# A delta-rule attention with a feed-forward layer on one core: loads of the attention moved between two weight loads in SyncE's queue

## The chip, the cores and the metric

One core of a Trainium2 chip. The metric is the device time of one execution in microseconds (us); of several runs the median is given. The profile is of one execution, taken by the hardware profiler.

## What is computed

A recurrent attention (the delta rule) over 4 sequences, 8 heads, 768 steps and head size 48, and behind it a feed-forward layer of 384 to 2048 to 384 with a leaky relu, on 3072 rows:

```python
for t in range(S):
    kt, vt, bt = (k_n[:, :, t], v[:, :, t], beta[:, :, t, None])   # k_n: k over its norm
    y[:, :, t] = np.einsum('bhd,bhde->bhe', q[:, :, t], state)
    v_old = np.einsum('bhde,bhd->bhe', state, kt)
    state = state + bt[:, :, :, None] * np.einsum('bhd,bhe->bhde', kt, vt - v_old)
...
h = x @ w_in
g = np.maximum(0.01 * h, h)
return (g @ w_out)
```

## The kernel before

The 768 steps are cut into 12 blocks of 64. Within a block the recurrence becomes products of matrices with the inverse of a triangular matrix, so that only the state goes from block to block. Each block is done in two groups (`g`) of two sequences. Blocks are numbered from 0 here as in the code; blocks 0 and 1 share one inverse.

The stages of a block `n`, each a generator: `gram(n)` loads `kq` (k and q, transposed, two loads for each group), multiplies k by k and k by q on TensorE (L306), copies the first product with ScalarE to `gs` (L310), stores the half-blocks of it that lie on the diagonal to a buffer `gd` in DRAM, four stores for each group (L314), and at the end reads `gd` back in another layout as `L`, two loads (L344). `inv` takes the norms from `L`'s diagonal on VectorE (`norms`, from L363) and eliminates step by step on VectorE (L387, L392); the inverse goes through DRAM (`td`, `tt`) and back (`rt`, `sq`), unless it is that of blocks 0 and 1. `solve(n)` applies it: `load` (with `merge_z`, TensorE's `pz`, L489), `tie`, `kt` (scales `v` on VectorE, L626), `step_w`, `step_y` (takes `q`) and `step_s` (the state into the next block's `v`). `ffn(n)` is the feed-forward layer, 16 pieces of 128 hidden units; it is the bulk of TensorE's work (L721, L712). From block 1 on its operands are split in a high and a low part, `xl` (L124), `gl` (L736) and the weights' lows (L189) being made by VectorE.

The weights come as eight loads of 1.5 MB, wr0 to wr7, each a "pair" of two pieces (`load_w(j)`). During block 0 each is packed by ScalarE (`pack`, L148), converted by VectorE (`conv`, L158 to L161), expanded by ScalarE (L168) and finished by VectorE (`final`, L175), and later split (`cast`, `lows`). Loads 4 to 7 wait for a memset on VectorE (L131), which writes to the same buffer and is placed behind a mark.

The order on every engine is chosen by a planner in the framework, which lets each engine take the earliest traced instruction that its own estimate of the times has ready. `with behind(name)` adds an edge: what is traced in it stays behind the instruction that `mark[name]` holds at that time, on that instruction's engine, without a wait. `mark["kq"]` orders SyncE's loads: before the change it is the last load of `qx` for blocks 0 and 1, from the first 12 us, until much later in the kernel. So all `kq`, `rk`, `rv`, `rq` loads (the tiles of k, v and q) are free to go as soon as their buffers are. `fetch(n, g)` issues the three loads of a group of block `n`. The buffers of `v` and `q` are four each (two blocks), those of `k` two (one block). For block 1 and block 2 `fetch` is called in `solve(n)`'s `load`, for later blocks at the end of the solve of the block before.

The core of the order by hand, at the end of the kernel's body: the first stages, then a loop over the 17 steps of each block's `ffn`, in which `work` lists weight steps by number (`load_w` of 6 and 7 in steps 2 and 4) and `weave_at` interleaves the other generators.

Of the kernel before, what the change touches and what calls it, by code (L numbers as in the profile page):

```python
# [12 lines left out]
U16 = mybir.dt.uint16  # L13
# [13 lines left out]
NGR = NSEQ // GS  # L27
# [20 lines left out]
def delta_moe_kernel(ctx: ExitStack, tc, kq0, kqT, kv, qT, beta, cst, w_all, out, nblk):  # L48
# [10 lines left out]
    nc = tc.nc  # L59
    DO = out.shape[1]  # L60
    NFC = w_all.shape[1] // (2 * DO)
    w16 = w_all.bitcast(U16)
# [25 lines left out]
    UP, DN = slice(0, D), slice(R0, P)  # L88
# [4 lines left out]
    def of(x, n, g):  # L93
        return ring[x][(n * NGR + g) % NR[x]]

    def tv(n, g):

        t = of("t", n, g)
        return t.rearrange("p y (c v) t -> p c y v t", c=2) if n < 2 else t.rearrange("p c (y v) t -> p c y v t", y=2)
# [16 lines left out]
    raws, mark = {}, {}  # L116

    def behind(name):

        return tc.issue_after(mark[name]) if name in mark else nullcontext()  # L120
# [5 lines left out]
    def load_w(j, gate=None):  # L126
        if j < NJ:
            raws[j] = raw = sb.tile([P, 8 * DO], F32, tag=f"w{j}", name=f"wr{j}", bufs=1)
            if gate:
                with behind(gate):  # L130
                    nc.vector.memset(raw[:, 0:1], 0.0)  # L131
            with behind("kq"):
                nc.sync.dma_start(raw.bitcast(U16), w16[:, 16 * DO * j + 1:16 * DO * (j + 1) + 1])

    def signs():
        nc.scalar.mul(neg, eye, -1.0)
# [13 lines left out]
    def after(inst):  # L150
        mark["gl"] = mark["dv"] = inst.ins
# [11 lines left out]
    def expand(j, gate, e=slice(0, 2)):  # L163

        g = parts[j][0]
        a, b = e.start * 2 * DO, e.stop * 2 * DO
        with behind(gate):
            nc.scalar.copy(g[:, a:b], g.bitcast(BF16)[:, 4 * DO + a:4 * DO + b])  # L168

    def final(j, e=slice(0, 2)):  # L170
        g, mid = parts[j]
        a, b = e.start * 2 * DO, e.stop * 2 * DO
        gi = g[:, a:b].bitcast(U32)
        with behind("dv"):
            after(nc.vector.scalar_tensor_tensor(gi, mid[:, a:b], 13, gi, ALU.logical_shift_right, ALU.bitwise_or))  # L175
        for e in range(e.start, e.stop):
            w32[2 * j + e] = g[:, e * 2 * DO:(e + 1) * 2 * DO]
# [19 lines left out]
    def need(gen, fn, n):  # L197
        while (fn, n) not in done:
            next(gen)
# [354 lines left out]
    LD = 2  # L554
    NSLOT = LD + 4

    def fetch(n, g):
        with behind("kq"):
            for i, x in enumerate("kv"):
                nc.sync.dma_start(of(x, n, g)[DN].rearrange("p h u t -> p (h u t)"), kv[n, g, i])  # L560
            nc.sync.dma_start(of("q", n, g)[UP].rearrange("p h u t -> p (h u t)"), qT[n, g])

    nts = {}

    def lengths(n):

        b, i = where[n]
        ps = ps_a.tile([P, 512], F32, tag="a", name=f"pn{n}")
        nc.tensor.matmul(ps[DN, 0:HS], nrm[b][i * 64:i * 64 + 64], eye0[i * 64:i * 64 + 64], start=True, stop=True)
        nt = nts[n] = sb.tile([P, NGR, 2, GU], F32, tag="nt", name=f"nt{n}", bufs=2)  # L570
        if n < 2:
            for y in range(2):
                nc.scalar.copy(nt[DN, :, :, y * NPAIR:(y + 1) * NPAIR],
                               ps[DN, y * GH:(y + 1) * GH].rearrange("p (g h v) -> p g h v", g=NGR, h=2))
        else:
            nc.scalar.copy(nt[DN].rearrange("p g h u -> p (g h u)"), ps[DN, 0:HS])
        if not n:
            for g in range(NGR):
                v = of("v", n, g)
                for u in range(GU):  # L580
                    for c in range(2):
                        nc.scalar.mul(v[DN, c, u], v[DN, c, u], nt[DN, g, c, u:u + 1])

    def solve(n):
        b = where[n][0]
        need(iv, inv, b)
        if n not in nts:
            with behind("po"):
                lengths(n)
        nt = nts.pop(n)  # L590

        def load(g):
            merge_z(n, g, tv(n, g))
            if 0 < n < 3:
                fetch(n, g)

        def tie(g):
            merge_u(n, g, tv(n, g))

        def heads(rows):  # L600

            return ((c, u, slice(c * 64, c * 64 + rows)) for u in range(GU) for c in (1, 0))

        def quarters():

            return ((c, u, e) for u in range(GU) for c in range(2) for e in range(2))

        def out_of(x, g, w):
            p = ps_a.tile([P, 512], F32, tag="a", name=f"{x}{n}_{g}")
            return p[:, 0:GU * w].rearrange("p (u t) -> p u t", u=GU)  # L610

        def kt(g):

            t, k, v = tv(n, g), of("k", n, g), of("v", n, g)
            if n:
                pv = out_of("pk", g, C)
                for c, u, r in heads(D):
                    nc.tensor.matmul(pv[r, u], k[DN, c, u], t[DN, c, u // NPAIR, u % NPAIR], start=True, stop=True)  # L618
                for c in range(2):
                    nc.scalar.mul(t[UP, c], pv[c * 64:c * 64 + D].rearrange("p (y v) t -> p y v t", y=2), -1.0)  # L620
            if not n:
                return
            for s in range(GS):
                us = slice(s * NPAIR, (s + 1) * NPAIR)
                with behind("gl"):
                    nc.vector.tensor_tensor(  # L626
                        v[DN, :, us], v[DN, :, us],
                        nt[DN, g, :, us].rearrange("p h (u o) -> p h u o", o=1).broadcast_to([C, 2, NPAIR, D]), ALU.mult)

        def step_w(g):  # L630
            t, v = tv(n, g), of("v", n, g)
            pv = out_of("pw", g, D)
            for c, u, e in quarters():
                a = c * C + e * HC
                nc.tensor.matmul(pv[a:a + HC, u], t[:, c, u // NPAIR, u % NPAIR, e * HC:(e + 1) * HC], v[:, c, u], start=True, stop=True)  # L635
            for c in range(2):
                d = nc.scalar.copy(v[DN, c], pv[c * 64:c * 64 + C])  # L637
            mark["rv"] = d.ins

        def step_s(g):  # L640
            k, v, v1 = of("k", n, g), of("v", n, g), of("v", n + 1, g)
            pv = out_of("pc", g, D)
            for c, u, r in heads(D):
                with nullcontext() if n else behind("ph"):
                    nc.tensor.matmul(pv[r, u], k[:, c, u], v[:, c, u], start=True, stop=True)  # L645
            for c in range(2):
                nc.scalar.copy(v1[UP, c], pv[c * 64:c * 64 + D])  # L647

        def step_y(g):

            qa, v = of("q", n, g), of("v", n, g)
            pv = ps_a.tile([P, 512], F32, tag="a", name=f"py{n}_{g}")
            for c, u, e in quarters():
                a = (c ^ (u // NPAIR)) * C + e * HC
                nc.tensor.matmul(pv[a:a + HC, u * D:(u + 1) * D], qa[:, c, u, e * HC:(e + 1) * HC], v[:, c, u], start=True, stop=True)  # L655
            ys[n, g] = y = sb.tile([P, DO], F32, tag="ys", name=f"ys{n}_{g}", bufs=3)
            mark["ys"] = nc.scalar.copy(y, pv[:, 0:DO]).ins
            if not n and not g:
                expand(0, "ys", slice(1, 2))

        stages = [(0, load), (1, tie), (LD, kt), (LD + 1, step_w), (LD + 2, step_y), (LD + 3, step_s)]
        if n in (0, nblk - 1):
            stages.remove((LD + 3, step_s))
        for s in range(NSLOT):
            for g in range(NGR):
                for at, stage in stages:
                    if at == s:
                        stage(g)
            if s == NSLOT - 1:
                done.add((solve, n))  # L670
                if 1 < n < nblk - 1:
                    for g in range(NGR):
                        fetch(n + 1, g)
                if n == 0:
                    columns(0)
                    yield
                    for g in range(NGR):
                        step_s(g)
            yield
# [102 lines left out]
    def weave(n, *streams):  # L782
        for gen, steps, a, b in streams:
            for i in range(steps):
                next(gen, None)
# [9 lines left out]
    for f in range(KA):  # L795
        load_w(f)
    for g in range(NGR):
        fetch(0, g)
    for f in range(KA, WEARLY):
        load_w(f)  # L800
# [10 lines left out]
    expand(0, "rv", lo)  # L811
    final(0, lo)
    conv(1)
    for j in (4, 5):
        load_w(j, "dv")
    weave(1, (sv, 2, 0, 1))
    next(gg)
    final(0, hi)
    work = {
        0: ((expand, 1, "xh"), (conv, 2)),  # L820
# [98 lines left out]
```

## Time and profile before

| | |
|---|---|
| time, median of 3 runs | 624.64 us (624.12 to 624.98) |
| profiled execution, its time | 623.75 us |
| its span in the profile | 622.0 us |
| TensorE matmul (PE) busy | 577.6 us, 93% |
| TensorE weight load (PEld) busy | 532.0 us, 86% |
| VectorE (DVE) busy | 431.3 us, 69% |
| ScalarE (ACT) busy | 329.9 us, 53% |
| GpSimd (POOL) busy | 10.7 us, 2% |

The shares are means over the whole span; the weight preparation and blocks 0 and 1 fill roughly the first 130 us. An engine's queue is in order: an instruction that waits holds up all behind it. SyncE (SP) only issues transfers. A transfer has a time from its issue to its landing, which includes its wait behind earlier ones.

### The profile page before, as it was taken

What the parts mean: (1) busy time and instruction counts of PE and PEld (TensorE: products, weight loads), DVE (VectorE), ACT (ScalarE), POOL (GpSimd) and SP (SyncE); (2) the same over time, 40 slices, a digit from 0 to 9 for tenths busy, and PEclk for the clock granted to TensorE, in tenths of its full rate; (3) what the DMA queues carried; (4) which work ended last, traced back from release to release, by engine and by line L of the source; (5) the groups of instructions that cost most, each with busy time, mean ns of one, the idle gap of its engine ahead of it and who ended that gap; (6) DMA issues with size and microseconds to landing.
All of it is one profiled execution on the core that took longest, in us unless ns stands there. A gap on an engine that the chain in (4) does not pass through costs nothing.

```text
span 622.0 us, 22298 instructions
## 1 busy us (share of the span) xinstructions
PE 577.6 (93%) x9122; PEld 532.0 (86%) x9122; DVE 431.3 (69%) x1949; ACT 329.9 (53%) x818; POOL 10.7 (2%) x17
## 2 busy tenths in 40 slices
PE   5287989899899989999999999999999999999996
PEld 4265767688888989999999999999999999999996
DVE  3999899979559948759759649749759559231221
ACT  3378886636445535545545545545555545454332
POOL 6000000000000000000000000000000000000000
PEclk9989999999999999999999999999999999999999
DMA  5986923261365560561561571570570540500101
GB/s 127 319 254 240 285 64 80 59 115 18 66 129 101 116 116 11 108 120 42 109 121 40 112 129 30 118 142 15 114 146 16 113 90 4 92 22 4 25 1 26
DMA packets 123430, 59.69 MB, mean 96 GB/s; under 512 B 111296, under 2 KB 114496, under 8 KB 122304
## 3 DMA queue, kind: packets, MB, share of 16 engines
q1 hardware_dynamic: 120576, 57.27, 41.7%
q10 hardware_dynamic: 2752, 0.98, 0.8%
q8 instruction: 72, 1.18, 0.8%
q14 instruction: 30, 0.25, 0.1%
HBM read 46.96 MB, written 11.27 MB: 94 GB/s over the span
## 4 chain that ended last, share of the span: by engine, by line
PE 75%; DVE 13%; DMA 4%; ACT 3%; issue 3%; SPq 2%; DVEq 0%; ACTq 0%
PE po L712 29%; PE ph L721 29%; PE pk L618 3%; PE pw L635 3%; DVE T L392 3%; DVE tmp L387 3%; PE py L655 3%; PE pc L645 2%; PE pg L306 2%; DVE w L189 1%; DMA sq<-tt 1%; PE pz L489 1%; PE px L690 1%; PE pu L489 1%; DMA kx<-in_kq 1%
## 5 line engine op out<-in xcount | busy, mean ns | idle before, releaser
L721 PE MATMUL ph<-xh,w 128*128 128x256 f32 x1056 | 204.9, 285 | 0.5 <-issue 0.5
L712 PE MATMUL po<-w,gh 128*128 128x384 f32 x704 | 179.1, 345 | 0.0
L736 DVE TENSOR_TENSOR gl<-ph,gh 128x256 fp32r<-128x256 f32 x176 | 73.9, 420 | 145.9 <-ACT ph L735 135.1
L721 PEld LDWEIGHTS ph<-xh,w 128*128 128x128 f32 x1056 | 168.6, 189 | 4.6 <-issue 3.7
L731 ACT ACTIVATE gh<-ph 128x256 fp32r<-128x256 f32 (+1 forms) x192 | 73.5, 385 | 173.2 <-PE ph L721 123.0
L721 PE MATMUL ph<-xl,w 128*128 128x256 f32 x528 | 148.7, 283 | 1.7 <-DVE xl L124 1.7
L712 PEld LDWEIGHTS po<-w,gh 128*128 128x128 f32 x704 | 121.8, 189 | 3.4 <-issue 2.0
L712 PE MATMUL po<-w,gl 128*128 128x384 f32 x352 | 113.5, 343 | 2.3 <-DVE gl L736 2.3
L392 DVE TENSOR_TENSOR T<-T,tmp 128x60 f32<-128x60 f32 (+35 forms) x661 | 112.3, 206 | 0.7
L387 DVE TENSOR_TENSOR tmp<-T,L 128x60 f32<-128x60 f32 (+35 forms) x661 | 111.8, 207 | 0.6
L721 PEld LDWEIGHTS ph<-xl,w 128*128 128x128 f32 x528 | 99.7, 189 | 2.7 <-DVE xl L124 2.1
L712 PEld LDWEIGHTS po<-w,gl 128*128 128x128 f32 x352 | 65.8, 189 | 3.8 <-DVE gl L736 2.9
L735 ACT ACTIVATE ph<-ph 128x256 f32<-128x256 f32 x176 | 67.0, 380 | 0.0
L323 DVE TENSOR_TENSOR rq<-pg,csb 64x256 f32<-64x256 f32 x80 | 33.8, 423 | 1.6
L620 ACT ACTIVATE rt<-pk 48x512 f32<-48x512 f32 x44 | 26.0, 591 | 7.4 <-PE pk L618 6.7
L647 ACT COPY rv<-pc 48x384 f32<-48x384 f32 x44 | 20.8, 474 | 12.3 <-PE pc L645 11.8
L721 PE MATMUL ph<-x,cg 128*128 128x256 f32 x96 | 22.8, 385 | 3.8 <-DVE cg L175 2.2
L721 PEld LDWEIGHTS ph<-x,cg 128*128 128x128 f32 x96 | 17.7, 190 | 8.4 <-DVE cg L175 3.7
L637 ACT COPY rv<-pw 64x384 f32<-64x384 f32 x48 | 22.7, 473 | 3.7 <-PE pw L635 2.5
L655 PEld LDWEIGHTS py<-rv,rq 128*32 128x32 f32 x1536 | 18.1, 109 | 6.6 <-issue 2.3
L655 PE MATMUL py<-rv,rq 128*32 128x48 f32 x1536 | 20.6, 207 | 3.0 <-ACT cg L168 1.4
L712 PE MATMUL po<-cg,gh 128*128 128x384 f32 x64 | 22.7, 493 | 0.0
(98 smaller groups left out, 578.6 us busy)
## 6 DMA issues: line engine op xcount, KB each, us to landing
wr<-in_w_all SPq DMA_DIRECT2D x8, 1536.0 KB, 13.7
kq<-in_kqT SPq DMA_DIRECT2D x40, 192.0 KB, 4.2
L<-gd SPq DMA_DIRECT2D x20, 256.0 KB, 4.0
rk<-in_kv SPq DMA_DIRECT2D x24, 192.0 KB, 3.8
rv<-in_kv SPq DMA_DIRECT2D x24, 192.0 KB, 4.2
rq<-in_qT SPq DMA_DIRECT2D x24, 192.0 KB, 3.6
out<-ob SPq DMA_DIRECT2D x46, 96.0 KB, 2.2
td<-T SPq DMA_DIRECT2D x40, 64.0 KB, 3.1
```

The lines of the kernel that those rows point to most:

```text
L323: nc.vector.tensor_tensor(qa[DN, c, b * NPAIR:(b + 1) * NPAIR], pv[b][r, 1], tri[r].rearrange("p (o t) -> p o t", o=1).broadcast_to([C, NP ...
L387: nc.vector.tensor_tensor(tv, t[:, :, j:j + 1].broadcast_to([P, k, w]), L[:, j, j + 1:].rearrange("p (o w) -> p o w", o=1).broadcast_to([P ...
L392: mark["steps"] = nc.vector.tensor_tensor(t, t, tv, ALU.subtract).ins
L620: nc.scalar.mul(t[UP, c], pv[c * 64:c * 64 + D].rearrange("p (y v) t -> p y v t", y=2), -1.0)
L637: d = nc.scalar.copy(v[DN, c], pv[c * 64:c * 64 + C])
L647: nc.scalar.copy(v1[UP, c], pv[c * 64:c * 64 + D])
L655: nc.tensor.matmul(pv[a:a + HC, u * D:(u + 1) * D], qa[:, c, u, e * HC:(e + 1) * HC], v[:, c, u], start=True, stop=True)
L712: i = nc.tensor.matmul(po[t][:, :DO], a[:, ts_], w, start=(f == 0 and k == 0), stop=(f == NFC - 1 and k + 1 == len(ways)))
L721: i = nc.tensor.matmul(ph, w[:, cc * P:(cc + 1) * P], a, start=(k == 0), stop=(k + 1 == len(ways)))
L731: i = nc.scalar.activation(gh, ph, AF.Prelu, alpha=0.01)
L735: i = nc.scalar.activation(ph, ph, AF.Prelu, alpha=0.01)
L736: mark["gl"] = nc.vector.tensor_tensor(gl, ph, gh.bitcast(F32), ALU.subtract).ins
```

## The change

A gated `load_w` (loads 4 to 7) now moves `mark["kq"]` to itself, so every load traced later under `behind("kq")` comes after it in SyncE's order. Load 5 is traced later than before: behind the `kq` loads of block 2 (`next(gg)`) and behind the `v` and `q` of block 1, whose `fetch` is moved here and moves the mark too. `solve(1)`'s `load` fetches only `k` now.

```diff
@@ load_w
             with behind("kq"):
-                nc.sync.dma_start(raw.bitcast(U16), w16[:, 16 * DO * j + 1:16 * DO * (j + 1) + 1])
+                d = nc.sync.dma_start(raw.bitcast(U16), w16[:, 16 * DO * j + 1:16 * DO * (j + 1) + 1])
+            if gate:
+                mark["kq"] = d.ins
@@ fetch
-    def fetch(n, g):
+    def fetch(n, g, what="kvq"):
         with behind("kq"):
-            for i, x in enumerate("kv"):
-                nc.sync.dma_start(of(x, n, g)[DN].rearrange("p h u t -> p (h u t)"), kv[n, g, i])
-            nc.sync.dma_start(of("q", n, g)[UP].rearrange("p h u t -> p (h u t)"), qT[n, g])
+            for x in what:
+                src = qT[n, g] if x == "q" else kv[n, g, "kv".index(x)]
+                d = nc.sync.dma_start(of(x, n, g)[UP if x == "q" else DN].rearrange("p h u t -> p (h u t)"), src)
+        return d
@@ solve
             if 0 < n < 3:
-                fetch(n, g)
+                fetch(n, g, "k" if n == 1 else "kvq")
@@ the order by hand
     conv(1)
-    for j in (4, 5):
-        load_w(j, "dv")
+    load_w(4, "dv")
     weave(1, (sv, 2, 0, 1))
     next(gg)
+    for g in range(NGR):
+        mark["kq"] = fetch(1, g, "vq").ins
+    load_w(5, "dv")
     final(0, hi)
```

## Rows read from the trace of the kernel before

**Rows 1.** Windows: stretch, us, busy PE PEld DVE ACT POOL, clock, DMA share, GB/s

```profile
78.00:80.00 2.00, 2.00 (x7) 1.04 (x8) 2.00 (x3) 1.80 (x3) 0.00 (x0) 1.00 0.12 39
...
113.00:130.00 17.00, 13.02 (x137) 11.06 (x136) 16.68 (x43) 7.88 (x21) 0.00 (x0) 1.00 0.49 106
```

**Rows 2.** Waits from 113 to 130 us: total us, times, longest us

```profile
PE po L712 <- DVE gl L736: 2.3, 2, 1.3
...
PE ph L721 <- DVE xl L124: 1.7, 2, 1.2
```

**Rows 3.** Timeline of SyncE's queue: start us, us, what is issued

```profile
47.66 2.62 SPq L561 DMA_DIRECT2D rq<-in_qT  x2
...
76.04 3.61 SPq L284 DMA_DIRECT2D kq<-in_kqT  x2
...
80.25 1.80 SPq L314 DMA_DIRECT2D gd<-gs  x4
```

**Rows 4.** DMA issues by line and window: duration ns, first and last start; us to landing

```profile
L133 SPq DMA_DIRECT2D wr<-in_w_all x2: 347/366/384, 52.9 to 53.3; - x2
DMA to landing us min/median/max: 6.0/8.3/10.6
...
L133 SPq DMA_DIRECT2D wr<-in_w_all x1: 334/334/334, 62.4 to 62.4; - x1
DMA to landing us min/median/max: 16.9/16.9/16.9
...
L284 SPq DMA_DIRECT2D kq<-in_kqT x1: 327/327/327, 28.5 to 28.5; - x1
DMA to landing us min/median/max: 15.0/15.0/15.0
...
L561 SPq DMA_DIRECT2D rq<-in_qT x1: 310/310/310, 42.9 to 42.9; - x1
DMA to landing us min/median/max: 4.2/4.2/4.2
...
L560 SPq DMA_DIRECT2D rk<-in_kv x2: 472/509/546, 58.5 to 59.7; - x2
L560 SPq DMA_DIRECT2D rv<-in_kv x2: 562/854/1147, 59.1 to 60.3; - x2
DMA to landing us min/median/max: 12.8/13.4/13.7
...
L314 SPq DMA_DIRECT2D gd<-gs x4: 329/446/1068, 73.0 to 75.0; - x4
DMA to landing us min/median/max: 6.2/6.8/7.5
...
L344 SPq DMA_DIRECT2D L<-gd x2: 457/520/584, 83.4 to 83.9; - x2
DMA to landing us min/median/max: 3.4/3.7/4.0
```

**Rows 5.** Timeline of VectorE: start us, us, line, operation, output and input

```profile
70.99 1.97 DVE L626 TENSOR_TENSOR rv<-rv,nt 64x384 f32<-64x384 f32 x4
...
90.38 0.12 DVE L363 TENSOR_SCALAR sr<-L 128x32 uint32<-128x32 uint32 x1
...
92.96 0.50 DVE L158 TENSOR_SCALAR cg<-cg 128x768 uint32<-128x768 uint32 x1
```

**Rows 6.** Timeline of ScalarE from 60 to 125 us: the packs of weights

```profile
61.25 1.60 ACT L148 COPY cg<-wr 128x1536 bf16<-128x1536 bf16 x1
...
72.87 1.60 ACT L148 COPY cg<-wr 128x1536 bf16<-128x1536 bf16 x1
...
90.39 1.60 ACT L148 COPY cg<-wr 128x1536 bf16<-128x1536 bf16 x1
```

**Rows 7.** Timeline of TensorE: start us, us, and the wait before it

```profile
68.45 1.10 PE L306 MATMUL pg<-kq 48*64 48x128 f32 x32
...
140.27 0.64 PE L489 MATMUL pz<-sq,gm 128*32 128x128 f32 x16 [0.18 <-DMA sq<-tt]
```

## Prediction

> **What bounds the kernel now.** I read the page's shares first: TensorE is busy 93% of the span, VectorE 69%, so after its start this is a TensorE kernel. The change touches only loads that are issued before 63 us, so I went to the stretches of the start. In the windows [rows 1] the reader is to see that from 113 to 130 us VectorE is full (16.68 of 17 us) while TensorE lacks 4.0 us. The waits of that stretch [rows 2] say for whom: VectorE's `gl` 2.3 us and `xl` 1.7 us, together the 4.0 us. So what VectorE loses on the way to 130 us, TensorE loses too, and a load counts only if it makes an instruction of a full engine wait.
>
> SyncE's timeline [rows 3] and the landings [rows 4] show how loads queue. The fifth weight pair (wr4) is issued at 52.9 and lands at 52.9 + 6.0 = 58.9, the sixth (wr5) at 53.3 + 10.6 = 63.9, the eighth (wr7) at 62.4 + 16.9 = 79.3. Block 3's two `kq` loads at 76.04 take 3.61 us to issue: the second goes out as wr7 lands, eight issues ahead of it on SyncE, so about eight transfers are open at a time. Of the four `gd` stores of block 2's first half the last is issued at 75.0 and lands at 75.0 + 6.2 = 81.2: a store of 32 KB took 6 us, because wr7 was ahead of it. The second half's `gd` is issued from 80.25, and L344, which reads all of it back as `L`, at 83.4 and 83.9; `L` has landed at 83.9 + 4.0 = 87.9. VectorE first reads it at 90.38 (L363) [rows 5]. So block 2's `L` has 90.4 - 87.9 = 2.5 us to spare.
>
> **The change part by part.** *Removed from 28 to 47 us:* four `kq` and the `v` and `q` of block 1, eight loads of 192 KB, the first issued at 28.5, the last landed at 42.9 + 4.2 = 47.1 [rows 4]. Their consumers come after 68 us (below), and the weight pairs wr2 and wr3 are ahead of them in the queue. Gain 0. *Removed ahead of wr4:* the two `rq` of block 2 [rows 3]; they are issued by 50.3, 2.6 us before wr4, which waits for its memset on VectorE and not for them. Gain 0.
>
> *wr4 with its memset:* nothing ahead of it changes, so it still leaves at about 52.9. It is now followed by small loads instead of a pair. wr4 alone took 6.0 us, and with up to two of the dearer steps below (0.9 us each, so 1.8) mixed into it, it lands at 60.7 at worst. ScalarE packs it at 61.25 [rows 6]: hidden, with half a us of cover in that case.
>
> *Inserted behind wr4:* the eight loads. Their price in the queue comes from landings [rows 4]: as they stood, the first `kq` at 28.5 + 15.0 = 43.5 and the last `rq` at 47.1, seven steps, 0.51 us each; the four `rk` and `rv` between two weight pairs, 58.5 + 12.8 = 71.3 to 60.3 + 13.7 = 74.0, three steps, 0.90 us each. I keep both ends, though the second position is the one that the moved loads get. All eight have landed by 60.7 + 8 x 0.90 = 67.9 at the latest. TensorE takes `kq` at 68.45 (L306) [rows 7], VectorE takes `v` at 70.99 (L626) [rows 5], and `q` is taken later still: hidden, by little at the upper price.
>
> *wr5 behind them:* a pair behind a pair took 63.9 - 58.9 = 5.0 us. It lands at 58.9 + 4.1 + 5.0 = 68.0 to 60.7 + 7.2 + 5.0 = 72.9. ScalarE packs it at 72.87 [rows 6]: hidden, with no cover left at the worst end, where it would cost what it is late.
>
> *What follows wr5:* `load_w` now moves the mark, so all that is traced later under `behind("kq")` comes after wr6 or wr7. The `rv` pair of block 2, now ahead of wr7, and its `rq` pair, now ahead of wr4, both go behind wr7, and still ahead of block 3's first `kq` pair and of the `gd` stores. So the queue in front of the first `gd` holds 8 + 2 = 10 more loads than now (the `rv` pair changes its place inside it). At 0.51 to 0.90 us these are 5.1 to 9.0 us, and the last `gd` of the first half lands at 86.3 to 90.2 instead of 81.2. From there to `L` it is 87.9 - 81.2 = 6.7 us now. Of these, the 2.2 us up to L344's start at 83.4 could be saved if the second half's stores are no longer behind the first half's: so `L` lands at 86.3 + 6.7 - 2.2 = 90.8 at the earliest, and at 93.0 to 96.9 without that saving. L363, now at 90.38, then waits 0.4 us at the least, 2.6 to 6.5 without the saving, in the middle 4.5.
>
> Behind L363 stand, on VectorE, the preparation of block 2's inverse, the conversion of wr7 (L158 at 92.96 [rows 5]) and the elimination up to 130 us, with the `xl` and `gl` for which TensorE waits. The price is smaller if the planner, which orders each engine by an estimate of its own, puts the conversion ahead of L363. That needs ScalarE's pack of wr7, done at 90.39 + 1.60 = 91.99 [rows 6], so VectorE is idle for 92.0 - 90.4 = 1.6 us even so; conversion and final steps fill the rest. Between 1.6 (filled) and 4.5 us (not filled) the trace doesn't choose, and I take the middle, 3.0. All of it reaches the end: `pz` of block 2 on TensorE, at 140.27, waited 0.18 us for its `sq` [rows 7], so that inverse has no slack behind it either.
>
> By the rows a small store behind wr7 landed only after wr7 (81.2 against 79.3). The Trainium skill, "DMA: Bandwidth & Descriptors", section "Queues, rings and completion order", says that completion is not first-in first-out for one issuing engine, by which `gd` could overtake loads and the time stay at 624.6; here landing followed issue. By the fit in its section "Anatomy of one DMA" a load of 196,608 bytes costs 0.45 us beyond the fixed part, an estimate of 4.5 us for ten, where the rows give 5.1 to 9.0.
>
> **The sum.** The profiled execution took 622.0 of span and 1.75 around it, 623.75; plus 3.0 it is 626.75. The median of before, 624.64, stands 0.89 above that execution, so the forecast is 627.6.
>
> **The rivals.** *No change:* `L` lands by about 91, because the ten loads cost less than now or `gd` lands ahead of some of them; or the planner keeps both engines full around the gap. For it: from 78 to 80 us the queue moves 39 GB/s [rows 1], room that some of the ten may use. Against it: 5.1 us at the least against 2.5 to spare. Time 624.6. *Faster:* with `L` late, the planner puts block 2's elimination behind block 1's `xl`, weight lows and `gl`; TensorE's waits [rows 2] shrink, and half of the 4.0 us gives 622.6. It decides on whether block 2's `pz` can move back with other products in front of it: now it has 0.18 us to the bad, so both orders would have to change. *A pack waits:* wr4 or wr5 is late for ScalarE, and block 1's weights behind it; a miss of 2 us gives 626.6. Only the upper prices make it. That SyncE's order stays as it was I give no chance, since the marks fix it.
>
> **How the numbers follow.** Two timings of this kernel are told apart from about 0.2%, 1.25 us. The forecast (`L` late) gets 0.54, a pack late 0.05, no change 0.24, faster 0.17. So slower 0.59, same 0.24, faster 0.17. The forecast's own range is 624.6 plus 1.6 to 6.5: 626.2 to 631.1. The range over all cases goes through no change into the smaller gains, 623.4, and leaves out the last half us of the prices, 630.6.
>
> **What would show it.** On SyncE: wr4 near 52.9, then the eight loads, wr5 by 60. wr7 lands after 82, the last `gd` of the first half after 86, `L` after 90.8. VectorE waits 1.6 us or more in front of L363, or has L158 ahead of it, and `pz` comes later by as much. The prediction is wrong if the last `gd` of the first half lands before 84, if L363 runs at about 90 without a wait, or if TensorE's 4.0 us of waits are gone.

## The result, and the profile after

The changed kernel takes 633.87 us (median of 4 runs, 631.53 to 635.39), beside 624.51 for the kernel before in the same set of runs: ratio 1.0133, 95% interval 1.0098 to 1.0167, or 6.1 to 10.4 us. It is slower, as forecast, but by three times the 3.0 us forecast, and outside the range. The profiled execution took 634.1 us with a span of 632.3 (before: 623.75 and 622.0), so the traces differ by 10.3 us. On VectorE, ScalarE, TensorE and GpSimd the instructions stand in the same order as before; only SyncE's order differs. All differences below are thus of waiting, not of a new plan. The new lines shift the numbers of the others by two or three (L363 is now L365, L344 is L346, L314 is L316).

SyncE's timeline of the kernel after, against [rows 3] (start us, us, what is issued):

```profile
53.08 0.33 SPq L133 DMA_DIRECT2D wr<-in_w_all  x1
53.46 2.04 SPq L286 DMA_DIRECT2D kq<-in_kqT  x4
...
59.73 0.31 SPq L563 DMA_DIRECT2D rq<-in_qT  x1
60.56 1.38 SPq L133 DMA_DIRECT2D wr<-in_w_all  x2
63.58 1.40 SPq L563 DMA_DIRECT2D rk<-in_kv  x2
65.44 0.33 SPq L133 DMA_DIRECT2D wr<-in_w_all  x1
...
77.65 1.91 SPq L286 DMA_DIRECT2D kq<-in_kqT  x2
80.18 8.56 SPq L316 DMA_DIRECT2D gd<-gs  x4
88.84 0.86 SPq L286 DMA_DIRECT2D kq<-in_kqT  x2
89.80 2.68 SPq L316 DMA_DIRECT2D gd<-gs  x4
94.73 1.10 SPq L346 DMA_DIRECT2D L<-gd  x2
```

The order is the one that the diff writes. wr5 leaves at 60.56, not at 53.3. The first half's four `gd` stores, issued within 2.0 us before (73.0 to 75.0 in [rows 4]), are spread over 8.56 us, and `L` is issued at 94.73 instead of 83.4.

The landings of these issues after, against [rows 4] (duration of the issue in ns, first and last start; then us from issue to landing):

```profile
L133 SPq DMA_DIRECT2D wr<-in_w_all x1: 328/328/328, 53.1 to 53.1; - x1
DMA to landing us min/median/max: 6.6/6.6/6.6
...
L286 SPq DMA_DIRECT2D kq<-in_kqT x2: 412/417/422, 53.5 to 53.9; - x2
DMA to landing us min/median/max: 7.0/7.3/7.5
...
L133 SPq DMA_DIRECT2D wr<-in_w_all x1: 333/333/333, 65.4 to 65.4; - x1
DMA to landing us min/median/max: 21.1/21.1/21.1
...
L316 SPq DMA_DIRECT2D gd<-gs x4: 303/309/330, 80.2 to 88.4; - x4
DMA to landing us min/median/max: 2.7/3.5/10.3
...
L346 SPq DMA_DIRECT2D L<-gd x2: 457/524/590, 94.7 to 95.2; - x2
DMA to landing us min/median/max: 3.6/3.9/4.2
```

wr4 lands at 53.1 + 6.6 = 59.7, wr7 at 65.4 + 21.1 = 86.5 (before 79.3), the last `gd` of the first half at 88.4 + 2.7 = 91.1 (before 81.2), `L` at 95.2 + 4.2 = 99.4 (before 87.9). The first two `kq` land at 60.5 and 61.4, and wr5 and wr6, each eight issues behind one of them, leave at 60.56 and 61.5: again eight transfers are open at a time, and never more in any trace of this case. The limit is the program's own: in the traces all transfers of SyncE and ScalarE take turns at the same eight completion semaphores, and each issue waits until the transfer that used its semaphore before has landed.

What the full engines make of it. VectorE's timeline after, against [rows 5] (in brackets the idle time ahead of the instruction, and what ended it):

```profile
90.20 0.48 DVE L416 MEMSET T<- 128x512 f32 x1
99.51 0.19 DVE L365 TENSOR_SCALAR sr<-L 128x32 uint32<-128x32 uint32 x1 [8.82 <-DMA L<-gd]
```

The waits of the kernel after from 85 to 135 us (total us, times, longest):

```profile
ACT sq L376 <- DVE sr L371: 9.7, 1, 9.7
...
DVE sr L365 <- DMA L<-gd: 8.8, 1, 8.8
PE py L658 <- ACT rv L640: 8.8, 1, 8.8
```

TensorE's timeline before and after, and after once more at block 2's `pz` (before: 140.27, [rows 7]):

```profile
94.51 0.28 PE L655 MATMUL py<-rv,rq 128*32 128x48 f32 x4
94.72 2.85 PE L712 MATMUL po<-cg,gh 128*128 128x384 f32 x8
```

```profile
93.25 1.58 PE L638 MATMUL pw<-rv,rt 128*32 128x48 f32 x128
103.64 0.38 PE L658 MATMUL py<-rv,rq 128*32 128x48 f32 x4 [8.81 <-ACT rv L640]
103.95 4.59 PE L715 MATMUL po<-cg,gh 128*128 128x384 f32 x8
...
149.77 0.64 PE L491 MATMUL pz<-sq,gm 128*32 128x128 f32 x16 [0.46 <-DMA sq<-tt]
```

The three waits are one chain. VectorE stands 8.82 us before its first read of `L`; ScalarE's `sq` (L376) needs that result and stands in ScalarE's order ahead of block 1's `rv` copies (L640); TensorE's `py` needs those copies. So TensorE loses the time at 95 us already, within a few us of VectorE, and not first through `xl` and `gl` of 130 us. From there on everything is later by about as much: `py` by 9.1 us, `pz` of block 2 by 9.5 (149.8 against 140.27).

The chain that ended last, of the kernel after, says the same from the end backwards (start us, us, what):

```profile
54.39 9.13 DMA kq<-in_kqT
63.58 15.65 DMA rk<-in_kv
79.25 11.00 DMA kq<-in_kqT
91.21 3.32 DMA gd<-gs
95.24 4.17 DMA L<-gd
```

From 54 to 99 us that chain runs through SyncE's queue alone: a moved `kq`, a load of block 2, one of block 3, then `gd` and `L`.

Windows of the kernel after (stretch, us, then busy us of PE, PEld, DVE, ACT, POOL with instruction counts; TensorE's granted clock; DMA share; GB/s):

```profile
58.00:66.00 8.00, 7.71 (x30) 5.68 (x31) 7.11 (x12) 7.62 (x12) 0.00 (x0) 1.00 1.05 229
66.00:72.00 6.00, 6.00 (x113) 4.69 (x112) 4.31 (x4) 5.80 (x9) 0.00 (x0) 1.00 0.98 391
...
122.00:139.00 17.00, 13.28 (x137) 11.19 (x136) 16.68 (x42) 8.33 (x21) 0.00 (x0) 1.00 0.47 95
```

From 58 to 66 us mostly loads of 192 KB move, with the DMA engines full and 229 GB/s; from 66 to 72 us the weight pair brings 391. The last row is the stretch of [rows 1], 9 us later: VectorE is full for the same 16.68 us, and TensorE lacks 3.7 us where it lacked 4.0.

### The profile page after: what moved, and what is told of

Same layout as the page of the kernel before. It is cut to its first block, busy times and chain, and to the rows that moved or that the text cites. A ratio compares the mean times of both kernels' runs of the same rounds, so it can differ in the third digit from the quotient of the medians.

```text
span 632.3 us, 22296 instructions
## 1 busy us (share of the span) xinstructions
PE 580.1 (92%) x9122; PEld 533.7 (84%) x9122; DVE 431.7 (68%) x1949; ACT 329.7 (52%) x818; POOL 10.7 (2%) x17
## 4 chain that ended last, share of the span: by engine, by line
PE 71%; DVE 12%; DMA 10%; SPq 2%; issue 2%; ACT 1%; DVEq 0%; ACTq 0%
PE po L715 28%; PE ph L724 28%; DMA kq<-in_kqT 3%; PE pk L621 3%; DMA rk<-in_kv 3%; DVE T L394 3%; DVE tmp L389 3%; PE pw L638 2%; PE py L658 2%; PE pc L648 2%; PE pg L308 2%; DMA sq<-tt 1%; DVE w L191 1%; PE pz L491 1%; PE px L693 1%
## 5 line engine op out<-in xcount | busy, mean ns | idle before, releaser
L658 PE MATMUL py<-rv,rq 128*32 128x48 f32 x1536 | 21.1, 212 | 9.4 <-ACT rv L640 8.8
L640 ACT COPY rv<-pw 64x384 f32<-64x384 f32 x48 | 22.7, 473 | 3.9 <-PE pw L638 2.8
L715 PE MATMUL po<-cg,gh 128*128 128x384 f32 x64 | 24.4, 523 | 0.0
```

Source lines behind the costliest of these rows:

```text
L715: i = nc.tensor.matmul(po[t][:, :DO], a[:, ts_], w, start=(f == 0 and k == 0), stop=(f == NFC - 1 and k + 1 == len(ways)))
```

## The experiments

Four theories. *A*: each further load of 192 KB ahead of the first `gd` delays `L` by a constant 1.15 us (11.5 us over ten), and what exceeds the 2.5 us of slack is lost. *B*: one group of the moved loads is itself late or in the way. *C*: what counts is the number of transfers, about eight being open, not their bytes. *S*: eight small loads in a row fill the open places, so that the weight pairs behind them are issued late. Under each edit stand its expectation and its result; the table puts all of them side by side (us; a ratio is to the kernel before in the same set of runs, whose median was 624.51 to 626.21, so ratios are to be compared rather than medians). The landings and waits are those of one traced execution each.

| kernel | loads more ahead of `gd` | wr7 lands | `L` lands | wait for `L` | median | ratio, 95% interval |
|---|---|---|---|---|---|---|
| before | 0 | 79.3 | 87.9 | 0 | 624.51 | |
| e7_before_L | -4 | 75.7 | 88.8 | 0 | 624.75 | 0.9982 (0.9951 to 1.0013) |
| e3_block2_late | +2 | 77.0 | 89.9 | 0 | 624.67 | 0.9994 (0.9966 to 1.0023) |
| e2_kq_only | +4 | 81.3 | 90.3 | 0 | 623.57 | 0.9976 (0.9948 to 1.0004) |
| e6_vq_only | +4 | 80.5 | 89.8 | 0 | 623.92 | 0.9978 (0.9948 to 1.0009) |
| e4_after_L | +4 | 84.5 | 91.0 | 0.50 | 624.55 | 0.9984 (0.9964 to 1.0005) |
| e12_six | +6 | 83.2 | 91.6 | 0.97 | 624.83 | 0.9987 (0.9960 to 1.0014) |
| e1_block2_free | +8 | 87.8 | 98.1 | 7.77 | 632.00 | 1.0089 (1.0055 to 1.0124) |
| after | +10 | 86.5 | 99.4 | 8.82 | 633.87 | 1.0133 (1.0098 to 1.0167) |
| e8_halves | +10 in bytes | 86.9 | 98.9 | 8.57 | 634.45 | 1.0157 (1.0127 to 1.0187) |
| e9_wr5_between | +10 | 87.4 | 99.0 | 8.24 | 631.97 | 1.0105 (1.0048 to 1.0161) |
| e10_fill | +10 | 85.7 | 99.2 | 0.32 | 629.31 | 1.0052 (1.0029 to 1.0075) |
| e11_fill_before | 0 | 80.2 | 88.8 | 0 | 630.14 | 1.0061 (1.0034 to 1.0088) |
| e5_gd_L_off | other queues | 84.5 | 99.3 | | 645.91 | 1.0334 (1.0304 to 1.0364) |

Down to e9_wr5_between every kernel has the kernel before's order on the four compute engines.

**e1_block2_free**: the kernel after, with block 2's `v` and `q` free to go where they stood.

```diff
-        mark["kq"] = fill(1, qx, (nc.sync, nc.sync)).ins
+        mark["kq"] = mark["qx"] = fill(1, qx, (nc.sync, nc.sync)).ins
...
     def fetch(n, g, what="kvq"):
-        with behind("kq"):
+        with behind("qx" if n == 2 else "kq"):
```

> The changed kernel, but block 2's v and q are free as before (q ahead of wr4, v ahead of wr7); VectorE's, ScalarE's and TensorE's orders are those of before. Theory A (every further load ahead of block 2's gd stores delays L; in the changed kernel ten loads moved L's landing from 87.9 to 99.4, 1.15 us each, and 2.5 us of it are slack): eight loads, L at about 97.1, VectorE waits 6.5 to 7 us for L, time 624.5 + 6.7 = 631.2. Theory B (the loss belongs to one group of moved loads, kq or v and q, being late itself): 633.9, as the changed kernel, since both groups are still moved.

Most of the loss stays: 632.00, near A's 631.2 (ten runs from 627.20 to 634.89; the trace is of the longest). It doesn't need block 2's `v` and `q` behind wr7; the eight loads behind wr4 suffice. VectorE's timeline of this kernel:

```profile
98.20 0.19 DVE L365 TENSOR_SCALAR sr<-L 128x32 uint32<-128x32 uint32 x1 [7.77 <-DMA L<-gd]
```

**e2_kq_only**: the kernel before, with only block 2's four `kq` between wr4 and wr5.

```diff
...
     weave(1, (sv, 2, 0, 1))
+    old, mark["kq"] = mark["kq"], mark["ld4"]
     next(gg)
+    mark["kq"], mark["pre5"] = old, mark["kq2"]
+    load_w(5, "dv")
...
```

(`load_w(5)` is ordered behind `mark["pre5"]`, and its call ahead of `weave` is gone; so in e6_vq_only and e12_six.)

> The kernel before with one part of the change: block 2's four kq loads behind wr4 and ahead of wr5; all else free as before. Theory A: four loads, L at about 92.5, a wait of about 2.1 us, 626.6. Theory B: all of the loss (633.9) if it is kq's, none (624.5) if it is that of v and q.

**e6_vq_only**: the kernel before, with only block 1's `v` and `q` between wr4 and wr5.

```diff
...
     next(gg)
+    old, mark["kq"] = mark["kq"], mark["ld4"]
+    for g in range(NGR):
+        mark["pre5"] = fetch(1, g, "vq").ins
+    mark["kq"] = old
+    load_w(5, "dv")
```

> The kernel before with the other part: block 1's two v and two q loads behind wr4 and ahead of wr5; kq early as before. Theory A: the same as the kq part alone, four loads, L at about 92.5, 626.6. Theory B: 633.9 or 624.5, the opposite of the kq part.

Neither half of the change costs anything: 623.6 and 623.9 against 624.5, within the measurement, and VectorE reads `L` at 90.45 and 90.58 without a wait. So no group is itself to blame, and B is refuted. But A expected 626.6 of both: four loads delay `L` by 2.4 and 1.9 us, not by 4.6. A's constant price is wrong for few loads. VectorE's timeline of e2_kq_only:

```profile
90.45 0.19 DVE L363 TENSOR_SCALAR sr<-L 128x32 uint32<-128x32 uint32 x1
```

**e3_block2_late**: the kernel before, with block 2's `v` and `q` behind wr7.

```diff
...
     def fetch(n, g):
-        with behind("kq"):
+        with behind("ld7" if n == 2 else "kq"):
```

(`mark["ld7"]` is the load of wr7)

> The kernel before with only block 2's v and q behind wr7 (q was ahead of wr4, v ahead of wr7): two loads more ahead of gd. Theory A: L lands at about 90.2 and stays inside its slack, VectorE waits 0 to 0.5 us, 624.5 to 625. If the slack counted from the trace is wrong, or each load costs a fixed part of the end time, 624.5 + 2 = 626.5.

No change, 624.67. The rest of the diff, `fetch` held behind wr7 for block 2, costs nothing alone. In this trace wr4 already leaves 1.1 us later (53.98), so of the 2.0 us at `L` only 0.9 are the loads'.

**e4_after_L**: the kernel after, with all that isn't needed soon (block 2's `v` and `q`, block 3's `kq`) behind `L`'s own load.

```diff
-            with behind("kq"):
+            with behind("L2" if n == 3 else "kq"):
...
+                if n == 2:
+                    mark["L2"] = i.ins
...
     def fetch(n, g, what="kvq"):
-        with behind("kq"):
+        with behind("L2" if n == 2 else "kq"):
```

> The changed kernel, but block 2's v and q and block 3's kq go behind the load of L; so the gd stores follow wr7 directly, with ten small loads ahead of them instead of sixteen (six in the kernel before). Theory A: gd lands 4 to 5 us after that of before for its first half, the second half is no longer behind kq, so L at 90 to 92.5, a wait of 0 to 2 us, 624.5 to 626.5. If the moved loads cost time in another way than by L's way through the queue, it stays near 633.9.

The whole loss is gone, 624.55 (0.9964 to 1.0005), though the eight loads still stand behind wr4. What the change costs is thus the time at which `L` comes through SyncE's queue; nothing else of it shows. The landing of wr7, and VectorE's timeline, of e4_after_L:

```profile
L133 SPq DMA_DIRECT2D wr<-in_w_all x1: 333/333/333, 65.7 to 65.7; - x1
DMA to landing us min/median/max: 18.8/18.8/18.8
```

```profile
91.03 0.19 DVE L367 TENSOR_SCALAR sr<-L 128x32 uint32<-128x32 uint32 x1 [0.50 <-DMA L<-gd]
```

Up to wr7 SyncE's order here is that of the kernel after, and wr7 is issued 0.3 us later, yet it lands at 84.5, before 86.5. Loads issued behind a pair can take part of its time: in the kernel after, from 82 to 86 us, with wr7 still under way, the DMA engines are full at 190 GB/s, about the rate of the small loads. How much that is stays open, since e10_fill, below, has the order of the kernel after on SyncE and its wr7 at 85.7. The Trainium skill, "DMA: Bandwidth & Descriptors", section "Queues, rings and completion order", says that transfers of one issuing engine needn't complete in order. Here they share the time, but in every trace of this case each engine's transfers landed in the order of their issue, so `gd` is not spared.

**e7_before_L**: the same, in the kernel before.

```diff
     def fetch(n, g):
-        with behind("kq"):
+        with behind("L2" if n == 2 else "kq"):
```

(and block 3's `kq` and the mark as in e4_after_L)

> The kernel before, with block 2's v and q and block 3's kq behind the load of L: four loads fewer ahead of the gd stores. Theory A: L lands earlier than 87.9, by up to 4.6 us, and nothing is gained since it already had 2.5 us to spare and VectorE's order is the same: 624.5 within 0.5. If VectorE's start on block 2 were set by L in some hidden way, 620 to 622.

With four loads fewer ahead wr7 lands 3.6 us earlier, but `L` no earlier (88.8). In the kernel before, the second half's `gd` waits for ScalarE, not for the queue. ScalarE's timeline of the kernel before:

```profile
79.58 0.64 ACT L310 COPY gs<-pg 128x256 f32<-128x256 f32 x2
```

That copy ends at 80.22, `gd` is issued at 80.25 [rows 3], and wr7 has landed at 79.3. So here the queue was no longer what held `L`. This is a likely reason, not tested by itself, why the first further loads cost less than the later ones.

**e8_halves**: the kernel after, with each of the eight moved loads in two halves: sixteen transfers, the same bytes.

```diff
-                    nc.sync.dma_start(t[b * R0:b * R0 + D].rearrange("p s u x t -> p (s u x t)"), kqT[n, g, b])
+                    to = t[b * R0:b * R0 + D].rearrange("p s u x t -> p (s u x t)")
+                    m = 2 if n == 2 else 1
+                    for a in range(m):
+                        s = slice(a * 1024 // m, (a + 1) * 1024 // m)
+                        nc.sync.dma_start(to[:, s], kqT[n, g, b][:, s])
```

(`v` and `q` likewise)

> The changed kernel with each of the eight moved loads in two halves: sixteen loads, the same bytes. Theory A as a price by bytes: L as in the changed kernel, 633.9 within 1. Theory C (the price is by transfers, because SyncE holds about eight open and waits for the one eight issues back): eight transfers more at 1 us each, up to 8 us more, 638 to 642.

`L` lands at 98.9 and the time is 634.45, as after: twice as many transfers cost no more. C is refuted: the bytes count, at the rate that such loads get, and not the number of transfers.

**e12_six**: the kernel before, with six loads (the four `kq`, one `v`, one `q`) between wr4 and wr5.

```diff
...
+    old, mark["kq"] = mark["kq"], mark["ld4"]
     next(gg)
+    mark["kq"] = mark["kq2"]
+    mark["pre5"] = fetch(1, 0, "vq").ins
+    mark["kq"] = old
+    load_w(5, "dv")
```

> The kernel before with six loads behind wr4 and ahead of wr5: block 2's four kq, and v and q of block 1's first group; all else free. Theory S: six fit into the open transfers, wr5 leaves at once, L at 90.5 to 91.5, VectorE waits 0 to 1 us, 624.5 to 625.5. Theory A alone: six times 1.15 us, L at 94.8, a wait of 4.4 us, 629.

**e9_wr5_between**: the kernel after, with wr5 between the four `kq` and the `v` and `q`.

```diff
...
     next(gg)
+    mark["kq"] = mark["kq2"]
+    load_w(5, "dv")
     for g in range(NGR):
         mark["kq"] = fetch(1, g, "vq").ins
-    load_w(5, "dv")
```

> The changed kernel with wr5 put between the four kq and the four v and q loads: the same loads ahead of gd, the same compute orders. Theory S (eight small loads in a row fill the about eight open transfers, so wr5 can't be issued before the first of them lands at 60.5, and from 58 to 64 us only small loads move, at some 210 GB/s): wr5 leaves by 56, wr7 and L land 2 to 3 us earlier, L at about 96.5, time 631 to 632. Theory A alone (1.15 us for every load ahead, wherever it stands): L at 99.4, 633.9.

Six loads give no measurable loss (624.83, a wait of 0.97 us), as S said and against A's 629. But the trace of e9_wr5_between speaks against S: wr5 leaves early, as meant, and `L` lands at 99.0, not at 96.5. VectorE's timelines of e12_six and of e9_wr5_between, and SyncE's of e9_wr5_between:

```profile
91.69 0.19 DVE L363 TENSOR_SCALAR sr<-L 128x32 uint32<-128x32 uint32 x1 [0.97 <-DMA L<-gd]
```

```profile
99.07 0.19 DVE L365 TENSOR_SCALAR sr<-L 128x32 uint32<-128x32 uint32 x1 [8.24 <-DMA L<-gd]
```

```profile
55.90 0.39 SPq L133 DMA_DIRECT2D wr<-in_w_all  x1
...
69.80 0.35 SPq L133 DMA_DIRECT2D wr<-in_w_all  x1
```

The second row is wr7. It leaves only when wr5, eight issues ahead of it, has landed (55.9 + 13.8 = 69.7), and wr7 then lands at 87.4, `L` at 99.0. In this trace the order among the loads only moves the place at which the issue stands. The time does not settle it: 631.97 is what S named, but the interval, 1.0048 to 1.0161, holds the kernel after's 1.0133 too, and the traced execution took 635.43, the longest of four.

**e10_fill** and **e11_fill_before**: one number of the planner's table, which puts block 2's norms and elimination later in the program, in the kernel after and, as a control, in the kernel before.

```diff
-IV, GG = ((9, 17), (6, 17), (6, 17), (2, 17)), ((2, 4), (1, 2), (1, 2))
+IV, GG = ((13, 17), (6, 17), (6, 17), (2, 17)), ((2, 4), (1, 2), (1, 2))
```

> The changed kernel with the norms and the elimination of block 2 traced four steps later, so that on VectorE the conversion of wr7 (2.6 us) and the last two final steps (3.5 us) stand ahead of L363's wait; SyncE's order as in the changed kernel. If the loss is VectorE's idle time alone, 8.8 - 6.1 = 2.7 us of it are left: 624.5 + 2.7 = 627.2. If L's delay costs through the end of block 2's inverse whatever fills the gap, 632 or more.

> The control to the run with the later norms: the kernel before with the same later tracing. VectorE was full there, so filling has nothing to fill: 624.5 within 1.5. If the later norms delay block 2's inverse against TensorE's pz (0.18 us of wait in the kernel before), 626 to 628.

VectorE now has the conversion of wr7 and two final steps ahead of its read of `L`. With that, `L` lands as late as after (99.2) and costs nothing: 629.31, between its two forecasts, against 630.14 for the control, whose VectorE comes to the same read only at 99.12 too. VectorE's timeline and the waits (85 to 135 us) of e10_fill:

```profile
99.26 0.19 DVE L365 TENSOR_SCALAR sr<-L 128x32 uint32<-128x32 uint32 x1 [0.32 <-DMA L<-gd]
```

```profile
PE po L715 <- DVE gl L739: 3.2, 1, 3.2
```

But this order has its own price: 1.0061 (1.0034 to 1.0088) in the control, more than either of its forecasts, with 3.9 us of TensorE's waits for `gl`. So "filled", in the prediction's words, costs about 3 us in this form (1.0052, against the 626.21 of its set): more than the 1.6 of the prediction, and far less than the change with the gap left open.

**e5_gd_L_off**: the kernel after, with block 2's `gd` stores issued by ScalarE and `L` by GpSimd, to leave SyncE's queue.

```diff
-            (nc.scalar if n == GS * NGR else nc.sync).dma_start(
+            (nc.scalar if n == 2 or n == GS * NGR else nc.sync).dma_start(
...
-                    i = nc.sync.dma_start(Lh[b0][r * 64:(r + 1) * 64]...
+                    i = (nc.gpsimd if n == 2 else nc.sync).dma_start(Lh[b0][r * 64:(r + 1) * 64]...
```

> The changed kernel with block 2's gd stores issued by ScalarE and L's load by GpSimd, past SyncE's queue; the planner moves some instructions of block 1 in consequence. Theory A as an order within SyncE's queue: gd lands within 3 us of its issue, L by 88, no wait at L363, 624.5 to 626. If instead the transfers of all queues share the engines in order of arrival, gd and L still wait behind the moved loads and 630 or more stays.

A's expectation, 624.5 to 626, failed by 20 us, and the cost goes far beyond the other branch's 630. ScalarE's timeline of e5_gd_L_off:

```profile
79.13 7.64 ACTq L316 DMA_DIRECT2D gd<-gs  x4
86.82 0.38 ACT L734 ACTIVATE gh<-ph 128x256 f32<-128x256 f32 x1 [12.35 <-DMA rq<-in_qT]
```

ScalarE took 7.64 us to issue four stores, and did no work for 12.35 us in all, until a load of SyncE's queue had landed. The reason is in the program: ScalarE's stores take their turn at the same eight semaphores as SyncE's transfers, and the second store, issued at 84.46, had to wait for wr7 (65.3 + 19.2 = 84.5). The compute orders moved as well, so not all of the 645.91 is this wait. The Trainium skill, "DMA: Bandwidth & Descriptors", section "Issuing engines are not separate DMA queues", says that transfers of all issuing engines run on the same 16 DMA engines and interleave, and that a second issuing engine saves only the time of issuing; the first of these stores, issued at 79.13, landed 9.3 us later, which agrees. That even the issuing took longer comes from the shared semaphores.

## Why the prediction was right in its direction and wrong in its size

**Right.** The place and the mechanism: ten more loads ahead of the first `gd`, `L` late, VectorE standing before L363. The removals gained nothing and the moved loads were in time for their readers: wr4 landed at 59.7 (60.7 at worst was forecast), the last moved load at 67.9 (the bound was 67.9), wr5 at 60.6 + 10.8 = 71.4 (68.0 to 72.9), ahead of ScalarE's pack at 73.09. wr7 came after 82 (86.5). The rival of a late pack did not come: in e4_after_L wr5 lands no earlier (60.4 + 11.4 = 71.8) and nothing is lost.

**Wrong: three terms of the sum were too small**, against `L`'s 8.8 us of wait where 3.0 were forecast.

1. *The price of a load in the queue*, 0.51 to 0.90 us. The last `gd` of the first half came 91.1 - 81.2 = 9.9 us later, 0.99 us per load on average; at the middle price, 0.705, ten loads gave 7.05. This is 2.9 us, the largest term. The price is not constant: four loads put `L` off by 2.4 and 1.9 us, six by 3.7. The upper price was called the likelier one, and then the middle was used. The rate was to be read in the trace of before: from 66 to 70 us, where block 2's `rk` and `rv` move, it shows

```profile
66.00:70.00 4.00, 4.00 (x105) 3.22 (x104) 2.56 (x2) 3.86 (x5) 0.00 (x0) 1.00 1.10 201
```

   (windows, same columns): DMA engines full at 201 GB/s, and 196,608 bytes at that rate are 0.98 us. The estimate of 4.5 us for ten that the prediction drew from the Trainium skill, "DMA: Bandwidth & Descriptors", section "Anatomy of one DMA", was farther off still: that section is headed as one on the path of transfers that GpSimd issues, and SyncE's ten took 9.9 us.
2. *The leg from there to `L`*, taken as 6.7 us with up to 2.2 to be saved. It grew to 99.4 - 91.1 = 8.3, 1.6 us more, and nothing was saved. Most of it is the second half's `gd`: before, it left as soon as ScalarE's copy was done (80.25); now it left only behind the first half and block 3's second `kq` pair (89.80), and its last store landed at 91.2 + 3.3 = 94.5, 3.4 us after the first half's instead of 2.0 (81.6 + 1.6 = 83.2). `L` itself is issued 0.2 us after that landing in both kernels, since it reads what `gd` wrote.
3. *The middle between "filled" and "not filled"*, which took 4.5 us to 3.0. The orders did not change at all, so it was "not filled" in full, 1.5 us. (e10_fill, which fills the gap by another order, is the cheaper case, but at 3 us and not at 1.6.)

Together 2.9 + 1.6 + 1.5 = 6.0, and 3.0 + 6.0 is 9.0, near the 8.8 measured. The forecast's way to the end, "all of it reaches the end", held: `pz` came 9.5 us later, and the whole 10.3. The way was another, ScalarE's `sq` ahead of `rv`, so TensorE lost the time at once.

**The rivals.** *No change* held in the prediction a true part: some of the loads use room in the queue. Up to six did (e2, e6, e12), eight and ten didn't. *Faster*, by a new order, had nothing for it: the planner's orders stayed.

**Open.** Why the price jumps between six and eight loads. wr5's landing moves evenly (63.9 before, 67.5 with the four `kq`, 69.4 with six, 71.3 and 71.4 with eight: about 0.9 us each), but `L` moves by 3.7 us with six and by 10.2 with eight. From e12_six to e1_block2_free `L` lands 6.5 us later: 1.9 of them are wr5's landing, 2.7 lie between the landings of wr5 and wr7, and 1.9 between wr7 and `L`. In the middle part the same transfers move, mostly wr6, wr7 and block 2's four loads, with the DMA engines full but at different rates. Windows of e12_six and of e1_block2_free from wr5's to wr7's landing (same columns):

```profile
69.40:83.20 13.80, 13.80 (x152) 10.27 (x144) 13.39 (x21) 11.82 (x21) 0.00 (x0) 1.00 1.02 291
```

```profile
71.30:87.80 16.50, 15.42 (x199) 11.38 (x197) 16.01 (x27) 13.30 (x21) 0.00 (x0) 1.00 0.97 236
```

What makes them slower there, no run here separates. The two traces also stand at opposite ends of their kernels' ten times (623.09 of 623.09 to 628.38, and 634.89 of 627.20 to 634.89), so a part may be scatter; that there is a step the ratios show, 0.9987 and 1.0089. Whether more than eight semaphores would have changed anything was not tried.

## What to carry to other kernels

Before a load is moved in an ordered queue, follow everything behind it to the first small transfer on which a full engine waits, and price each moved load by the rate of the window in which loads of its kind fill the DMA engines, not by the mean of two spacings. Slack at that transfer decides: here four or six loads fit and eight or ten did not, and putting what isn't urgent behind the small transfer gave the whole loss back. An engine's fixed order carries such a wait to the others at once, so look at what stands behind the waiting instruction on each engine, not only on its own.

## What the runs showed of the hardware

- Loads of 192 KB into 48 or 64 partitions move 201 to 229 GB/s with the DMA engines full (66 to 70 us before, 58 to 66 us after), the weight pairs around 391 (66 to 72 us after).
- In every trace of this case each engine's transfers landed in the order of their issue: a 32 KB `gd` store behind full loads took 6.2 us before and 10.3 us after, and 1.6 with little ahead of it.
- Loads issued behind a pair can move before it has landed (190 GB/s from 82 to 86 us, with wr7 in flight). wr7 took 18.8 us where `gd` stores followed it, 21.1 and 19.7 us (after, e10_fill) where four more loads came first.
- Not of the hardware: that eight transfers are open at a time, on SyncE and ScalarE together. The program has eight semaphores for them.
- In its wait of 8.8 us TensorE's granted clock fell, and it then ran at the lower of its two levels. Windows of the kernel after:

```profile
98.00:104.00 6.00, 0.36 (x5) 0.24 (x5) 4.17 (x17) 2.05 (x6) 0.00 (x0) 0.50 0.01 1
104.00:107.00 3.00, 3.00 (x7) 1.79 (x6) 2.99 (x5) 0.71 (x2) 0.00 (x0) 0.50 0.05 11
```

  The granted clock is 0.50, 1.2 GHz, until about 107.5 us. The eight `po` at 103.95 took 4.59 us, 2.85 in the kernel before; yet TensorE's delay grew only from 9.1 us at `py` to 9.5 at `pz`. Most of this was hidden: before, `py` waited 1.1 us in all for ScalarE's later `rv` copies (L637), and after it did not.
